# A fused attention and mixture-of-experts kernel: longer weight rows, early weights spread over the row tiles, and another order of expert loads

## The chip, the cores and the metric

The kernel runs on one core of a Trainium2 chip. The metric is device time in microseconds (us) of one execution; lower is better.

## The reference

Chunked attention feeds a mixture of experts with a capacity. The shapes are q, k, v: 8 x 8 x 576 x 64; x: 4608 x 512; w1: 8 x 512 x 1024; w2: 8 x 1024 x 512; capacity 80; all in float32.

```python
scores = scale * np.matmul(q_c, k_c.transpose(0, 1, 2, 4, 3))   # chunks of 64
attn = softmax(scores)
x = np.matmul(attn, v_c)                     # as 4608 rows of 512
logits = x @ w_gate
expert_idx = np.argmax(logits, axis=1)
gate_w = softmax(logits)[its own expert]
out = np.zeros((N, D))
for e in range(8):
    tok_idx = the 80 rows of expert e with the largest gate_w
    h = np.maximum(x[tok_idx] @ w1[e], 0.0)
    out[tok_idx] = gate_w[tok_idx, None] * (h @ w2[e])
```

So at most 640 of the 4608 rows of the output are not zero, but all 32 MB of expert weights (4 MB an expert) have to come in, and all of the output (9.4 MB) has to be written.

## The kernel before

**Attention.** The 4608 rows are 36 row tiles of 128. The loop at L1043 is software pipelined by hand: in turn i it does `scores(i)` (L387), `probs(i - 1)` (L420), `values(i - 2)` (L431), `finish(i - 2)` (L497) and `xtrans(i - 3)` (L520). Loads of q and k (`load_qk`, L376, 0.5 MB a tile, 7 buffers) and v (`load_v`, L369, 5 buffers) stand on SyncE's queue (SP), which issues in program order: what waits there holds up all that stands behind it. Every four tiles x is written to a scratch array `xs` in DRAM from GpSimd's queue (POOL).

**Lists.** For each expert the kernel finds a threshold, ranks the kept rows and makes a list of row numbers. For experts 0 and 1 a first list is made from tiles 0 to 23 alone (`first_list`, L792). Three one-hot tiles `ohS` (L843) on VectorE (DVE) are multiplied with `comp` in 24 small matmuls on TensorE (PE) into `liS` (`pe_list`, L852); `rows_` (L859) reads the row numbers from it and gathers 128 rows of `xs` by an indirect DMA (`gather`, L174). That is group 0. Its transposes (L928) and its first and second products with the weights of experts 0 and 1 (`first_group`, L922, tiles `h0` and `y0`) fill PE while the other lists are made after the loop. `first_q` and `pe1` are queues of small steps, of which the loop does one now and then (`burst`, L330; `step_one`, L318).

**Experts.** The other lists are five groups of 128 slots, each of four chunks of 32 slots, in `CHUNKS` (L46): group 1 holds experts 0 and 2, group 2 experts 1 and 3, group 3 experts 4 and 5, group 4 experts 5 and 6, group 5 experts 6 and 7. `place` (L148) makes the row numbers: `gi1` for group 1, then `gi2` for the other four. `experts` (L203) gathers the rows of each group, and for each does `xpose` (transposes), `layer1` in two halves (L222: 32 matmuls each, the instruction line is L185 in `product1`), `hpose` and `layer2` (64 matmuls, L193 in `product2`). Its order on PE from group 2 on is: first half of layer 1 of group r, `hpose` of r-1, `xpose` of r+1, second half of layer 1 of r, layer 2 of r-1. The result is scaled on DVE (L252) and scattered to the output by an indirect DMA (`store`, L198); the stores wait for each other and for all `clear`s (L287), nine DMAs of 1 MB that write zeros over the output.

**Weights.** `w1` of an expert is loaded as 128 partitions x 4 rows of 4 KB. `w2` is loaded as 128 partitions x 8 rows of 2 KB. The weights of experts 0 and 1 come in eight pieces of 1 MB (numbers 0 to 3: expert 0, first weights in two halves, then second weights; 4 to 7: expert 1), issued in the turns that the table `EARLY` (L42) gives (`early_weights`, L964). After the loop the DMA `hold` (L1094) waits for `tS`, which GpSimd makes behind the first gather's issue (L886), so that no later weights are issued before that gather. Then follow the loads of experts 2 to 7 and the clears (`part`, L1289; `ahead`, L1300; L1318 to L1323). `part(3, 1)` waits for a DVE copy into the buffer (L1295), which itself waits for `gi2` and stands on DVE behind the scaling of group 0.

**Buffers.** The pool `wp` has two buffers each for first and second weights (experts 0 and 1, then 5 and 6); `wp2` has six for either kind (experts 2, 3, 4, then 7). A load into a used buffer waits for the matmuls that read it last. `room` (L1282) chooses the pool:

```python
pool = wp if e in (5, 6) else wp2
for e, l in {0: ((3, 1), (4, 0), (4, 1)), 1: ((5, 0),),
             2: ((5, 1),), 3: ((6, 1), (7, 1))}.get(r, ()):
```

Here l = 0 is an expert's first weights and l = 1 its second. In turn 2 the last four clears, (6, 0) and (7, 0) follow.

Of the kernel before, what the change touches and what calls it, by code (L numbers as in the profile page):

```python
# [8 lines left out]
F32 = mybir.dt.float32  # L9
BF16 = mybir.dt.bfloat16  # L10
I32 = mybir.dt.int32
# [6 lines left out]
P = 128  # L18
# [5 lines left out]
NT = 9  # L24
# [14 lines left out]
LAG = 2  # L39
HOT = 8  # L40

EARLY = {6: [0], 14: [1], 28: [2, 3], 29: [4], 30: [5], 31: [6], 32: [7]}  # L42
VLOGITS = {28: (0,), 29: (1,), 33: (2, 3)}
FIRST = 24
FS = 64
# [22 lines left out]
def attention_moe(ctx: ExitStack, tc: tile.TileContext, qk, vv, v8, vt, wg, w1, w2, cap, cst, hst, out):  # L68
# [26 lines left out]
    slot_oob = cp.tile([P, NR], F32, name="slot_oob")  # L95
    flag_i = cp.tile([P, 1], I32, name="flag_i")

    def tiles_w(pool, e, tag=""):
        one = pool is not wp
        return (pool.tile([P, 4, FF], F32, name=f"w1_{tag}{e}", tag="w" if one else "w1"),  # L100
                pool.tile([P, 8, DM], F32, name=f"w2_{tag}{e}", tag="w" if one else "w2"))

    def load_w(pool, e, tag=""):
        a, b = tiles_w(pool, e, tag)
        nc.sync.dma_start(a, w1[e].rearrange("(c p) f -> p c f", p=P))
        nc.sync.dma_start(b, w2[e].rearrange("(c p) d -> p c d", p=P))
        return a, b

    mp = ctx.enter_context(tc.tile_pool(name="slots", bufs=1))
# [184 lines left out]
    with ExitStack() as actx:  # L294
# [35 lines left out]
        def burst(most=8):  # L330

            for _ in range(most):
                step_one(first_q)
# [458 lines left out]
        def first_list():  # L792
# [5 lines left out]
            c1S, pnS, thS, _ = const8("c1S"), const8("pnS"), const8("thS"), const8("rest", P)  # L798
            mS, iS, pS = (small(x, (2, FIRST), BF16) for x in ("mS", "iS", "pS"))
            tS = S['tS'] = small("tS", (2, FIRST))  # L800
            hot1 = []
            go = {}

            def emitted(nm, fn):
# [36 lines left out]
            def one_hot(j):  # L841
                oh = wk.tile([P, P, HOT], BF16, name=f"ohS{j}", tag="qk", bufs=NB)
                v.tensor_tensor(  # L843
                    oh.rearrange("p (e s) r -> p e s r", e=2),
                    S['io_s'].rearrange("p (e s) r -> p e s r", e=2),
                    pS[:, :, None, HOT * j:HOT * j + HOT].to_broadcast([P, 2, FS, HOT]),
                    op=ALU.is_equal)
                hot1.append(oh)
                if len(hot1) == FIRST // HOT:
                    emitted("list", pe_list)  # L850

            def pe_list():  # L852
                Z['liS'] = li = pa.tile([P, 6, 2], F32, name="liS", tag="acc")
                for rt in range(FIRST):
                    nc.tensor.matmul(li, lhsT=hot1[rt // HOT][:, :, rt % HOT],
                                     rhs=comp[:, rt, :, 0:2],
                                     start=rt == 0, stop=rt == FIRST - 1)

            def rows_():  # L859
# [104 lines left out]
        def early_weights(n):  # L964

            e, c = divmod(n, 4)
            if c == 0:
                weights[e] = tiles_w(wp, e)
            j = c % 2
            w, src, m = ((weights[e][0], w1, 2), (weights[e][1], w2, 4))[c // 2]  # L970
            nc.sync.dma_start(
                w[:, m * j:m * j + m],
                src[e].rearrange("(c p) f -> p c f", p=P)[:, m * j:m * j + m])

        with tc.manual_schedule():
            load_qk(0)
# [66 lines left out]
            for i in range(RT - 1):  # L1043
                if i == 6:
                    late_constants()
                S['i'] = i
                scores(i)
                j = i - 4
                due = j >= 0 and j % 4 == 3
                if due:  # L1050
                    gate_mm(j - 3, 4)
                    gate_copy(j - 3, 4)
                if i >= 1:
                    probs(i - 1)
                    if i == 1:
                        warm_up(8)
                if i >= 2:
                    values(i - 2)
                    burst()
                    finish(i - 2)  # L1060
                pe_slot()
                if i == 34:
                    step_one(pe1)
                if i >= 2:
                    for r in VLOGITS.get(i, ()):
                        value_logits(r)
                if due:
                    gate_sum(j - 3, 4)
                    gates.append((group_done, (j // 4,)))
                if i >= 3:  # L1070
                    xtrans(i - 3)
                pe_slot()
                if i < 33:
                    step_one(pe1)
                if i == 21:
                    nc.sync.dma_start(S['vT'], vt)
                if i == 25:
                    nc.sync.dma_start(vh, v8)
                if i == 30:
                    S['io_s'] = wk.tile([P, P, HOT], BF16, name="io_s", tag="qk", bufs=NB)  # L1080
                    nc.scalar.copy(S['io_s'].rearrange("p (e s) r -> p e s r", e=2),
                                   io_b[:, None, 0:FS, None].to_broadcast([P, 2, FS, HOT]))
                if i >= 2 and i - 2 + NB < RT:
                    load_qk(i - 2 + NB)
                if i >= 2 and i - 2 + NV < RT:
                    load_v(i - 2 + NV)
                for n in EARLY.get(i, ()):
                    early_weights(n)
# [3 lines left out]
            assert 'xg0' in S  # L1092
            hold = mp.tile([P, 2], F32, name="hold")
            nc.sync.dma_start(hold, S['tS'][:, 0, 0:2])  # L1094
            scores(35)
            gate_mm(28, 4)
            gate_copy(28, 4)
# [125 lines left out]
                select(e)  # L1223
            ahead_first(1)
            pl1, gi1 = place(mp, ps2, "g", sel_part, cb, "c", CHUNKS[:1])
            ahead_first(4)
            halves_ = slice(0, FS), slice(FS, P)
            nL = small("nL", (1,))
            for e, q in enumerate(halves_):
# [46 lines left out]
    with tc.manual_schedule():  # L1276
        with ExitStack() as ectx:
# [4 lines left out]
            def room(e, l):  # L1282

                w = weights.setdefault(e, [None, None])
                pool = wp if e in (5, 6) else wp2
                w[l] = pool.tile([P, *((4, FF), (8, DM))[l]], F32, name=f"w{l + 1}_{e}",
                                 tag=f"w{l + 1}" if pool is wp else "w")

            def part(e, l, after=None):  # L1289
# [3 lines left out]
                w = weights[e][l]  # L1293
                if after is not None:
                    nc.vector.tensor_copy(w[:, 0, 0:1], after)  # L1295
                nc.sync.dma_start(w, (w1, w2)[l][e].rearrange("(c p) f -> p c f", p=P))

            stored = []

            def ahead(r, xg, scale, ys):  # L1300

                if r == 0:
                    ahead_first(RT)
                    scale(0, S_y0)
                for e, l in {0: ((3, 1), (4, 0), (4, 1)), 1: ((5, 0),),
                             2: ((5, 1),), 3: ((6, 1), (7, 1))}.get(r, ()):
                    part(e, l, S_gi2[:, 0:1] if (e, l) == (3, 1) else None)
                if r == 2:
                    for n in range(5, NT):
                        clear(n)  # L1310
                    part(6, 0)
                    part(7, 0)
                if r >= 2:
                    for j in sorted(set(ys) - set(stored)):
                        store(ys[j], si[:, j:j + 1])
# [2 lines left out]
            room(2, 1)  # L1318
            part(2, 0)
            part(2, 1)  # L1320
            for n in range(5):
                clear(n)
            part(3, 0)  # L1323
            experts(ep, pp, lambda r: gi1[:, 0:1] if r == 1 else gi2[:, r - 2:r - 1], si, gate_t,
                    weights.get, "c", CHUNKS, ahead)
# [139 lines left out]
def _arrays(q, k, v, moe_w_gate, moe_w1, moe_w2, moe_capacity):  # L1465
# [12 lines left out]
        e[..., 0:64].transpose(1, 4, 0, 3, 2).reshape(P, 4, 8, 64))  # L1478
    r["wg"] = np.ascontiguousarray(moe_w_gate)
    r["w1"] = np.ascontiguousarray(moe_w1)  # L1480
    r["w2"] = np.ascontiguousarray(moe_w2)
    r["cap"] = np.asarray(moe_capacity, np.int64).reshape(1).view(np.int32).reshape(1, 2)
    r["cst"] = _constants()
    r["hst"] = _hist()
# [18 lines left out]
```

## Time and profile before

| | |
|---|---|
| time, median of 3 runs | 262.15 us (262.05 to 265.08) |
| profiled execution, its own time | 262.55 us |
| its span (first to last instruction) | 260.8 us |
| TensorE busy | 232.0 us, 89% of the span |
| TensorE weight load busy (beside it) | 131.8 us |
| VectorE, ScalarE, GpSimd busy | 135.1, 77.6, 49.3 us |
| mean granted TensorE clock | 0.953 of 2.4 GHz |
| DMA traffic | 86.17 MB, mean 330 GB/s |

The profile is one execution, with all times in us from its first instruction. PE is TensorE's matmul, PEld its weight load, DVE VectorE, ACT ScalarE, POOL GpSimd, SP SyncE; a q behind an engine's name means its instruction queue, which issues DMAs. "Idle <-X" is the time for which the engine stood still just before an instruction, and what released it. A clock of 1.00 is 2.4 GHz and 0.50 is 1.2 GHz. MB and GB here are powers of ten, KB are 1024 bytes: a weight load of 2048 KB is 2.10 MB.

### The profile page before, as it was taken

How to read it: one execution, taken by the hardware profiler on the slowest of the kernel's cores; microseconds unless marked ns; L12 is line 12 of the kernel's file. 1: busy time of each engine (PE TensorE's matmuls, PEld its weight loads, DVE VectorE, ACT ScalarE, POOL GpSimd, SP SyncE). 2: the span in 40 equal slices, each digit the busy share in tenths (PEclk: the TensorE clock that was granted, in tenths of full speed). 3: DMA queues.
4: the chain of work that ended last, by engine and by line, in shares of the span. 5: the costliest groups of instructions: out<-in, count | busy, mean ns of one | idle time of the engine just before them, and what ended most of it. 6: DMA issues, size and time to landing. Idle time of an engine off the chain costs nothing. (4 is left out here: it accounts for less than half of the span.)

```text
span 260.8 us, 8075 instructions
## 1 busy us (share of the span) xinstructions
PE 232.0 (89%) x3441; PEld 131.8 (51%) x3441; DVE 135.1 (52%) x429; ACT 77.6 (30%) x167; POOL 49.3 (19%) x127
## 2 busy tenths in 40 slices
PE   7699999999999999999988866999779949999970
PEld 5576767676767678778543522333114213333310
DVE  4688796969696997889486683112102101121210
ACT  2134445455554357533453401111002002010000
POOL 4003130303030483014351016000000011110110
PEclk9999999999999999997799995899979979999996
DMA  7899999999999999999999999799899999910011
GB/s 243 275 385 316 371 410 412 357 393 409 406 355 374 405 371 362 330 415 398 399 374 402 407 412 410 240 403 392 329 322 406 412 418 396 381 52 0 3 38 36
DMA packets 32665, 86.17 MB, mean 330 GB/s; under 512 B 3375, under 2 KB 3631, under 8 KB 32368
## 3 DMA queue, kind: packets, MB, share of 16 engines
q1 hardware_dynamic: 28912, 72.69, 74.9%
q0 software_dynamic: 3424, 12.32, 11.8%
q10 hardware_dynamic: 288, 0.59, 0.8%
q8 instruction: 29, 0.48, 0.7%
q14 instruction: 12, 0.10, 0.1%
HBM read 65.40 MB, written 20.45 MB: 329 GB/s over the span
## 5 line engine op out<-in xcount | busy, mean ns | idle before, releaser
L185 PE MATMUL hc<-w,xtc 128*32 128x512 f32 x320 | 42.0, 645 | 6.7 <-DMA w<-in_w 6.7
L454 PE MATMUL o<-vb,pT 128*64 128x130 f32 x512 | 35.4, 279 | 0.1
L193 PE MATMUL yc<-w,htc 128*32 128x512 f32 x320 | 35.3, 592 | 0.0
L401 DVE TENSOR_REDUCE mx<-s 128x8 f32<-128x512 f32 x36 | 24.7, 687 | 12.8 <-PE s L395 12.7
L454 PEld LDWEIGHTS o<-vb,pT 128*64 128x64 f32 x512 | 27.6, 135 | 5.5 <-issue 4.2
L427 ACT ACTIVATE pT<-pt 128x512 f32<-128x512 f32 x36 | 21.5, 598 | 25.3 <-PE pt L425 25.0
L395 PE MATMUL s<-qk 64*64 64x64 f32 x1152 | 25.9, 227 | 3.2 <-issue 1.6
L185 PEld LDWEIGHTS hc<-w,xtc 128*32 128x32 f32 x320 | 10.8, 117 | 34.2 <-issue 25.6
L524 ACT COPY xT<-px 128x512 f32<-128x512 f32 x32 | 18.8, 586 | 26.5 <-PE px L416 26.3
L404 DVE TENSOR_TENSOR sm<-s,mx 128x512 f32<-128x512 f32 x36 | 24.8, 690 | 0.7
L482 DVE TENSOR_TENSOR x<-o,rc 128x512 f32<-128x512 f32 x36 | 24.8, 688 | 0.6
L425 PE MATMUL pt<-ct,sm 128*128 128x128 f32 x144 | 23.7, 287 | 1.1
L395 PEld LDWEIGHTS s<-qk 64*64 64x64 f32 x1152 | 20.9, 136 | 6.8 <-issue 2.6
L229 ACT ACTIVATE hsc<-hc 128x512 f32<-128x512 f32 x5 | 3.0, 598 | 65.7 <-PE hc L185 65.7
L199 POOL DMA_INDIRECT out<-ysc,si x6 | 5.9, 988 | 87.3 <-issue 46.9
L193 PEld LDWEIGHTS yc<-w,htc 128*32 128x32 f32 x320 | 10.3, 110 | 23.5 <-issue 23.5
L425 PEld LDWEIGHTS pt<-ct,sm 128*128 128x128 f32 x144 | 15.1, 140 | 11.8 <-issue 5.8
L494 POOL DMA_DIRECT2D xs<-x x8 | 6.7, 832 | 72.4 <-DVE keys L590 50.0
L246 DVE COPY htc<-hpc 128x512 f32<-128x512 f32 x5 | 3.5, 692 | 30.4 <-PE hpc L242 30.4
L252 DVE TENSOR_SCALAR ysc<-yc,gate 128x512 f32<-128x512 f32 x5 | 3.8, 751 | 27.4 <-PE yc L193 27.4
L416 PE MATMUL px<-ct,x 64*128 64x64 f32 x256 | 15.3, 238 | 0.1
L231 DVE TENSOR_SCALAR hsc<-hc 128x512 f32<-128x512 f32 x5 | 3.5, 691 | 20.5 <-PE hc L185 20.5
(218 smaller groups left out, 259.8 us busy)
## 6 DMA issues: line engine op xcount, KB each, us to landing
w<-in_w SPq DMA_DIRECT2D x12, 2048.0 KB, 16.1
qk<-in_qk SPq DMA_DIRECT2D x35, 512.0 KB, 7.7
out<-zero SPq DMA_DIRECT2D x9, 1024.0 KB, 14.8
vb<-in_vv SPq DMA_DIRECT2D x64, 130.0 KB, 6.8
xs<-x POOLq DMA_DIRECT2D x8, 1024.0 KB, 10.5
w<-in_w SPq DMA_DIRECT2D x8, 1024.0 KB, 13.4
vh<-in_v SPq DMA_DIRECT2D x1, 1168.0 KB, 7.8
vT<-in_vt SPq DMA_DIRECT2D x1, 1024.0 KB, 6.9
```

What stands on the lines that cost most here:

```text
L185: nc.tensor.matmul(h[o:o + 32, :], lhsT=xT[:, b, o:o + 32], rhs=getw(e)[0][:, b, 512 * f:512 * f + 512], start=(b == 0), stop=(b == 3), ti ...
L193: nc.tensor.matmul(y[o:o + 32, :], lhsT=hT[c // 4][:, c % 4, o:o + 32], rhs=getw(e)[1][:, c, :], start=(c == 0), stop=(c == 7), tile_posit ...
L395: nc.tensor.matmul(ps[64 * u:64 * u + 64, h, 64 * pr:64 * pr + 64], lhsT=t['q'][64 * h:64 * h + 64, pr, u, :], rhs=t['k'][64 * h:64 * h + ...
L401: nc.vector.tensor_reduce(mx, s8, axis=AX.X, op=ALU.max)
L404: nc.vector.tensor_tensor(sm.rearrange("p c h k -> p h c k" if T == 8 else "p c k h -> p h c k"), s8, mx[:, :, :, None].to_broadcast([P, 2 ...
L416: nc.tensor.transpose(pm[:, u, 64 * pr:64 * pr + 64], src(pr)[rows], ident[rows, rows])
L425: nc.tensor.transpose(pt[:, pr, :], sv[:, pr, :], ident)
L427: nc.scalar.activation(pT, pt, AF.Exp, scale=0.125)
L454: nc.tensor.matmul(po[64 * u:64 * u + 64, pr // 2, o:o + 130].rearrange("p (h x) -> p h x", h=2), lhsT=d['pT'][:, pr, 64 * u:64 * u + 64], ...
L482: nc.vector.tensor_tensor(t['x'][:, r, :].rearrange("p (m j e) -> p j m e" if T == 8 else "p (j m e) -> p j m e", j=2, m=4), U[i]['pov'][. ...
L494: nc.gpsimd.dma_start(xs[T * 512:T * 512 + 512].rearrange("(c p) d -> p c d", p=P), t['x'])
L524: nc.scalar.copy(t['xT'][:, :, P * r:P * r + P].rearrange("p a (u j) -> p a u j", u=2), pm)
```

## The change

1. The array `w2` is laid out in DRAM so that each partition's rows j and j+1 lie side by side: the same tile is loaded as 4 rows of 4 KB instead of 8 of 2 KB.
2. The table `EARLY` spreads the eight early pieces: expert 1's first weights (4 and 5) go to turns 18 and 24, its second weights (6 and 7) behind `hold`.
3. The 24 list products are issued in three parts of eight, each when its one-hot tile is made, ahead of `probs(33)`, `values(32)` and behind them.
4. A new DMA `held` on SP waits for `mark`, a copy of `gi1` on ACT; expert 3's first weights stand behind it. The wait of (3, 1) for `gi2` is gone, and one clear of the first five goes to the last.
5. The second weights of expert 5 go to a buffer of `wp2`, and the order of the last loads and clears is another.

```diff
-EARLY = {6: [0], 14: [1], 28: [2, 3], 29: [4], 30: [5], 31: [6], 32: [7]}
+EARLY = {6: [0], 12: [1], 18: [4], 24: [5], 28: [2], 30: [3], 35: [6, 7]}
...
+    def source(l, e):
+        return (w1[e].rearrange("(c p) f -> p c f", p=P) if l == 0 else
+                w2[e].rearrange("c p j d -> p c (j d)"))
+    def wide(l, t):
+        return t.rearrange("p (c j) d -> p c (j d)", j=2) if l else t
...
-                hot1.append(oh)
-                if len(hot1) == FIRST // HOT:
-                    emitted("list", pe_list)
+                if j == 0:
+                    Z['liS'] = pa.tile([P, 6, 2], F32, name="liS", tag="acc")
+                emitted("list", lambda: pe_list(j, oh))
...
                 scores(i)
+                if i == 34:
+                    step_one(pe1)
...
                 if i >= 2:
+                    if i == 34:
+                        step_one(pe1)
                     values(i - 2)
+                    if i == 34:
+                        step_one(pe1)
                     burst()
                     finish(i - 2)
                 pe_slot()
-                if i == 34:
-                    step_one(pe1)
...
             nc.sync.dma_start(hold, S['tS'][:, 0, 0:2])
+            for n in EARLY[35]:
+                early_weights(n)
...
             pl1, gi1 = place(mp, ps2, "g", sel_part, cb, "c", CHUNKS[:1])
-            ahead_first(4)
+            ahead_first(2)
+            mark = mp.tile([P, 1], I32, name="mark")
+            nc.scalar.copy(mark, gi1)
+            ahead_first(2)
...
-                pool = wp if e in (5, 6) else wp2
+                pool = wp2 if e not in (5, 6) or (e, l) == (5, 1) else wp
...
-                for e, l in {0: ((3, 1), (4, 0), (4, 1)), 1: ((5, 0),),
-                             2: ((5, 1),), 3: ((6, 1), (7, 1))}.get(r, ()):
-                    part(e, l, S_gi2[:, 0:1] if (e, l) == (3, 1) else None)
+                for e, l in {0: ((3, 1), (4, 0), (4, 1)), 1: ((5, 0), (5, 1)),
+                             2: ((6, 0), (6, 1), (7, 0))}.get(r, ()):
+                    part(e, l)
                 if r == 2:
-                    for n in range(5, NT):
+                    for n in range(4, NT):
                         clear(n)
-                    part(6, 0)
-                    part(7, 0)
+                    part(7, 1)
...
-            for n in range(5):
+            for n in range(4):
                 clear(n)
+            held = mp.tile([P, 1], I32, name="held")
+            nc.sync.dma_start(held, mark)
             part(3, 0)
...
-    r["w2"] = np.ascontiguousarray(moe_w2)
+    r["w2"] = np.ascontiguousarray(np.asarray(moe_w2).reshape(NE, 4, 2, P, DM).swapaxes(2, 3))
```

The order of SP's queue around `hold`, before (w1_1 is an array of first weights, here expert 1's; w2 second weights; qk the loads of q and k; out<-zero the clears):

```order
L971 DMA w2_0_542<-in_w2 128x4x512 x2
L385 DMA qk34_2251<-in_qk 128x1024
L971 DMA w1_1_2253<-in_w1 128x2x1024
L385 DMA qk35_2320<-in_qk 128x1024
L971 DMA w1_1_2253<-in_w1 128x2x1024
L971 DMA w2_1_2254<-in_w2 128x4x512 x2
L1094 DMA hold_2685<-tS_2165 128x2
```

and now:

```order
L977 DMA w2_0_542<-in_w2 128x2x1024
L394 DMA qk34_2254<-in_qk 128x1024
L394 DMA qk35_2320<-in_qk 128x1024
L977 DMA w2_0_542<-in_w2 128x2x1024
L1103 DMA hold_2683<-tS_2168 128x2
L977 DMA w2_1_1363<-in_w2 128x2x1024 x2
```

Six early pieces stood between tile 33's loads and `hold`; now two do, and two follow `hold`. The other two (w1_1) stand some ten tiles earlier.

SP's queue from expert 3's first weights to its end, before:

```order
L1296 DMA w1_3_3208<-in_w1 128x4x1024
L1296 DMA w2_3_3249<-in_w2 128x8x512
L1296 DMA w1_4_3252<-in_w1 128x4x1024
L1296 DMA w2_4_3254<-in_w2 128x8x512
L1296 DMA w1_5_3300<-in_w1 128x4x1024
L1296 DMA w2_5_3395<-in_w2 128x8x512
L290 DMA out_0<-zero_75 512x1x512 x4
L1296 DMA w1_6_3401<-in_w1 128x4x1024
L1296 DMA w1_7_3403<-in_w1 128x4x1024
L1296 DMA w2_6_3504<-in_w2 128x8x512
L1296 DMA w2_7_3506<-in_w2 128x8x512
```

and now:

```order
L1337 DMA held_3209<-mark_3092 128x1
L1310 DMA w1_3_3211<-in_w1 128x4x1024
L1310 DMA w2_3_3252<-in_w2 128x4x1024
L1310 DMA w1_4_3254<-in_w1 128x4x1024
L1310 DMA w2_4_3256<-in_w2 128x4x1024
L1310 DMA w1_5_3302<-in_w1 128x4x1024
L1310 DMA w2_5_3304<-in_w2 128x4x1024
L1310 DMA w1_6_3399<-in_w1 128x4x1024
L1310 DMA w2_6_3401<-in_w2 128x4x1024
L1310 DMA w1_7_3403<-in_w1 128x4x1024
L299 DMA out_0<-zero_75 512x1x512 x5
L1310 DMA w2_7_3410<-in_w2 128x4x1024
```

Expert 6's first weights stood behind four clears and now stand ahead of all that are left; the last clears move behind three more loads, and one clear more is among them.

PE's queue around the list products in turn 34, before (s34, pt33 and o32 are the scores, transposes and values of tiles 34, 33 and 32):

```order
L395 MATMUL s34_2576<-qk34_2251 64x64 x16
L425 MATMUL pt33_2597<-ct_64,sm33_2489 128x128 x4
L444 MATMUL o32_2611<-vh_118,pT32_2506 64x73 x16
L855 LDWEIGHTS ohS0_2517
L855 MATMUL liS_2636<-comp_77,ohS0_2517 128x12
```

and now:

```order
L404 MATMUL s34_2575<-qk34_2254 64x64 x16
L862 LDWEIGHTS ohS0_2515
L862 MATMUL liS_2517<-comp_77,ohS0_2515 128x12
...
L434 MATMUL pt33_2604<-ct_64,sm33_2487 128x128 x4
L862 LDWEIGHTS ohS1_2518
L862 MATMUL liS_2517<-comp_77,ohS1_2518 128x12
...
L453 MATMUL o32_2626<-vh_118,pT32_2504 64x73 x16
```

Sixteen of the 24 products move ahead of o32, and the last eight stay behind it.

## Rows read from the trace of the kernel before

**Rows 1.** The page: the span, and the costliest group of instructions
```profile
span 260.8 us, 8075 instructions
...
L185 PE MATMUL hc<-w,xtc 128*32 128x512 f32 x320 | 42.0, 645 | 6.7 <-DMA w<-in_w 6.7
```

**Rows 2.** Timeline, PE, expert stage: start, us taken, line, names, shape, count [idle <-releaser]
```profile
186.71 1.03 PE L185 MATMUL hc<-w,xtc 128*32 128x512 f32 x6
190.64 5.32 PE L185 MATMUL hc<-w,xtc 128*32 128x512 f32 x26 [2.90 <-DMA w<-in_w]
...
212.51 5.15 PE L185 MATMUL hc<-w,xtc 128*32 128x512 f32 x28 [3.81 <-DMA w<-in_w]
...
219.05 3.64 PE L185 MATMUL hc<-w,xtc 128*32 128x512 f32 x32
...
241.97 10.51 PE L193 MATMUL yc<-w,htc 128*32 128x512 f32 x96
```

**Rows 3.** Busy us (xcount) of PE, PEld, DVE, ACT, POOL; PE clock, DMA share, GB/s
```profile
60.00:101.00 41.00, 40.28 (x814) 29.90 (x810) 34.51 (x123) 21.57 (x49) 14.99 (x43) 1.00 1.02 388
...
164.00:168.00 4.00, 4.00 (x40) 1.30 (x36) 0.27 (x2) 0.46 (x1) 0.00 (x0) 0.95 0.66 177
187.00:190.00 3.00, 0.74 (x6) 0.00 (x0) 0.74 (x1) 0.00 (x0) 0.00 (x0) 1.00 0.73 193
...
195.20:207.00 11.80, 11.80 (x106) 4.31 (x108) 1.39 (x2) 1.77 (x3) 0.00 (x0) 1.00 1.05 409
208.00:212.00 4.00, 0.70 (x4) 0.00 (x0) 0.70 (x1) 0.00 (x0) 1.03 (x1) 1.00 1.02 414
212.20:215.60 3.40, 3.09 (x16) 0.79 (x20) 0.00 (x0) 0.00 (x0) 0.24 (x1) 0.50 1.03 421
224.00:227.00 3.00, 3.00 (x32) 0.91 (x28) 0.00 (x0) 0.00 (x0) 0.00 (x0) 1.00 1.05 388
```

**Rows 4.** Waits of SP's queue: who <- whom: us in total, times, longest
```profile
SPq L1296 <- PE yc L193: 17.6, 2, 11.1
...
SPq L1296 <- DVE w L1295: 13.1, 1, 13.1
```

**Rows 5.** Timeline, SP: `hold`, then (5, 0) and (5, 1)
```profile
125.82 0.51 SPq L1094 DMA_DIRECT2D hold<-tS  x1
...
171.57 4.21 SPq L1296 DMA_DIRECT2D w<-in_w  x1
...
186.90 0.37 SPq L1296 DMA_DIRECT2D w<-in_w  x1
```

**Rows 6.** DMA issues at 171.6 and at 186.9: count, size, us from issue to landing
```profile
w<-in_w SPq DMA_DIRECT2D x1, 2048.0 KB, 19.0
...
w<-in_w SPq DMA_DIRECT2D x1, 2048.0 KB, 9.9
```

**Rows 7.** Timeline, PE: the list products, and the first gather's transposes
```profile
121.65 1.65 PE L855 MATMUL liS<-comp,ohS 128*128 128x12 bf16 x24
...
131.62 0.63 PE L928 MATMUL xp<-ct,xg 128*128 128x128 f32 x4 [1.47 <-DMA xg<-xs,gi]
```

**Rows 8.** Waits of PE's attention loop for q and k, whole run
```profile
PE s L395 <- DMA qk<-in_qk: 1.4, 3, 0.6
```

**Rows 9.** Timeline, POOL: group 1's gather; the first, second and last store
```profile
152.08 1.10 POOL L176 DMA_INDIRECT xgc<-xs,gic  x1 [8.00 <-DVE some L1240]
...
208.29 1.03 POOL L199 DMA_INDIRECT out<-ysc,si  x1 [46.93 <-issue]
215.36 1.00 POOL L199 DMA_INDIRECT out<-ysc,si  x1 [6.05 <-DMA out<-ysc,si]
...
253.58 0.97 POOL L199 DMA_INDIRECT out<-ysc,si  x1 [5.89 <-DVE ysc L252]
```

**Rows 10.** DMA issues at 208.3 and at 230.7: stores, us from issue to landing
```profile
out<-ysc,si POOLq DMA_INDIRECT x1, 6.3
...
out<-ysc,si POOLq DMA_INDIRECT x1, 2.7
```

More of the change, by code (lines that the diff above doesn't have):

```diff
@@ L105, in load_w @@
         nc.sync.dma_start(a, w1[e].rearrange("(c p) f -> p c f", p=P))
-        nc.sync.dma_start(b, w2[e].rearrange("(c p) d -> p c d", p=P))
+        nc.sync.dma_start(wide(1, b), source(1, e))
         return a, b
@@ L800, in first_list @@
             tS = S['tS'] = small("tS", (2, FIRST))
-            hot1 = []
             go = {}
@@ L847, in one_hot, with pe_list @@
                     op=ALU.is_equal)
-                hot1.append(oh)
-                if len(hot1) == FIRST // HOT:
-                    emitted("list", pe_list)
[L852 to L856, printed above, removed]
+                if j == 0:
+                    Z['liS'] = pa.tile([P, 6, 2], F32, name="liS", tag="acc")
+                emitted("list", lambda: pe_list(j, oh))
+            def pe_list(j, oh):
+                for rt in range(HOT * j, HOT * j + HOT):
+                    nc.tensor.matmul(Z['liS'], lhsT=oh[:, :, rt % HOT], rhs=comp[:, rt, :, 0:2],
                                      start=rt == 0, stop=rt == FIRST - 1)
@@ L969, in early_weights @@
             j = c % 2
[L970 to L973, printed above, removed]
+            l = c // 2
+            nc.sync.dma_start(wide(l, weights[e][l])[:, 2 * j:2 * j + 2],
+                              source(l, e)[:, 2 * j:2 * j + 2])
         with tc.manual_schedule():
@@ L1295, in part @@
                     nc.vector.tensor_copy(w[:, 0, 0:1], after)
-                nc.sync.dma_start(w, (w1, w2)[l][e].rearrange("(c p) f -> p c f", p=P))
+                nc.sync.dma_start(wide(l, w), source(l, e))
             stored = []
```

## The prediction

> **What bounds the kernel now.** I read the page first: its costliest group is the first product, with 6.7 us of idle time in front of it, all on weight loads [rows 1]. PE is busy 89% of the span, so the next view is PE's timeline in the expert stage: where are those 6.7 us? In two places [rows 2]. The first half of layer 1 of group 3 stops after 6 of its 32 matmuls and waits 2.90 us for (5, 0). The first half for group 4 stops after 4 and waits 3.81 us for (6, 0). Each wait costs more than itself. An undisturbed half takes 3.64 us for 32 matmuls, so 26 would take 2.96; after the first wait they took 5.32, which is 2.36 more. The 28 after the second should take 3.19 and took 5.15, 1.96 more. The windows say why: from 212.2 to 215.6 the granted clock was 0.50, the 1.2 GHz level, after PE had stood still [rows 3]. The two stops therefore cost 5.26 and 5.77 us. From the second one PE runs on to 252.48 (241.97 + 10.51); then comes the last scaling and store at 253.58 [rows 9], and the span ends at 260.8.
>
> Why are the loads late? The windows show two holes in the stream of transfers: 177 GB/s at 164 to 168 and 193 at 187 to 190, beside 409 to 421 in full stretches [rows 3]. SP's waits name them: 13.1 us on the DVE copy in front of (3, 1), and 11.1 us (the longer of two) on layer 2 of group 1, whose buffer (5, 1) needs [rows 4]. (5, 0) was issued at 171.57 and landed 19.0 us later, at 190.6 [rows 5, 6]: it stood behind other transfers, so it is the stream that was late, not its issue. (6, 0) stood behind four clears.
>
> **The change part by part.** Sums are against the profiled execution (262.55 us, of which the span is 260.8). It lies 0.4 above the median of 262.15, so I take 0.4 off at the end.
>
> *Rows of 4 KB.* Loads of 4 KB rows moved at 414 GB/s, loads of 2 KB rows at 388 [rows 3]. A load of 2.10 MB then takes 5.07 us rather than 5.41. Four such loads (expert 1's to 4's) stand ahead of (5, 0): 1.3 us. The bounds are 0 and 1.4.
> The Trainium skill ("DMA: Bandwidth & Descriptors", Specifications) gives 512 B as the transfer from which a DMA reaches line rate. By that rule both forms would be equal and this term 0; the two windows differ by 26 GB/s, which speaks against it, though other transfers lay in them too. It is rival B.
>
> *Early weights.* Pieces 4 and 5, 2.1 MB, move into turns 18 and 24. PE is busy 40.28 of 41 us from 60 to 101, and the engines move 388 GB/s there [rows 3]. At 414 they could move 1.07 MB more; the other 1.03 MB, 2.5 us, must come out of what is loaded ahead, and seven buffers of 0.5 MB hold 3.5 MB. PE waited for q or k only 1.4 us in the whole loop [rows 8], so I cost it at nothing; what it costs without that cover is rival C.
> Only two pieces then stand between turn 28 and `hold`, so the queue runs empty before the first gather. Its 1.47 us wait on PE [rows 7] should mostly go: I take 1.2, between 0.3 (only the smaller part) and 1.47. The values of the last tile stand behind that gather's transposes on PE, so the final lists, group 1's gather (152.08, [rows 9]) and all of the expert stage move with it.
>
> *List products in three parts.* 16 of the 24 move ahead of o32. The 24 take 1.65 us [rows 7], so o32 and DVE's work behind it come up to 1.1 us later, and with them perhaps the list, the gather's issue and `hold`. The bounds are 0 (the products no longer wait for the third one-hot tile) and 1.1. I take 1.1: `hold` at 126.9 instead of 125.82 [rows 5], the first load behind it at 127.5.
>
> *The restart.* Behind `hold` an empty queue has to get going. No row shows this. Nearest from above: (5, 1), issued into the hole at 187, took 9.9 us [rows 6], which is 4.5 beyond 5.4 of moving. From below: a store of 0.26 MB on idle engines took 2.7 [rows 10], 2.1 beyond its 0.6. I take the middle, 3.3. Pieces 6 and 7 (2.10 MB, 5.1 us) then have landed at 127.5 + 3.3 + 5.1 = 135.9.
>
> *`held`, and (3, 1) without its cast.* `mark` is a copy of one column on ACT, which I cost at nothing: ACT is busy 77.6 of 260.8 us. `held` waits for it near 152, just before the gather's issue [rows 9], while two loads and four clears behind piece 7, 8.4 MB, keep the queue busy until 135.9 + 20.5 = 156.4; so I cost it at nothing too, and if the clears ran out earlier, each us of gap makes the later loads 1 us later. Queued behind it on SP are expert 3's loads and all later ones. The 13.1 us wait of (3, 1) goes, and the hole at 164 with it. The one clear that moves from the first five to the end is worth 2.6 us of stream ahead of (5, 0).
>
> *Buffers and order.* (5, 1) now needs the buffer of expert 2's first weights, which is free after layer 1 of group 1 rather than layer 2: the hole at 187 goes. (6, 0) comes second behind (5, 0), without clears between.
>
> *Sum.* From 135.9 to the landing of (5, 0) the engines move seven loads (14.68 MB), four clears (4.19), the last x rows (1.05) and five gathers (1.31): 21.2 MB. At 410 GB/s, as from 195.2 to 207 [rows 3], that is 51.8 us: (5, 0) lands at 187.7 instead of 190.6. PE comes to it at 187.74 − 1.2 = 186.5 and waits 1.2 instead of 2.90. It goes on 2.9 us earlier, and of the slow matmuls' 2.36 I take half back, 1.2 (bounds 0 and 2.36). The second stop goes altogether: (6, 0) lands two loads later, 187.7 + 10.2 = 197.9. PE needed it at 208.7 (212.51 − 3.81) before, some 204.6 now, so there are 6.7 us to spare. Sum: −2.9 − 1.2 − 5.8 = −9.9, that is 252.65 for a profiled execution, **252.3 us** against the median.
>
> What is late next? The stores, which wait for all clears. Behind (5, 0) come four loads and five clears, 13.63 MB: the last clear lands at 187.7 + 33.2 = 220.9. The first store, 1.0 us behind it, takes 6.3 beside the last load [rows 10] and 0.8 until the next is issued (215.36 − 208.29 − 6.3, [rows 9]); four more at 2.7 + 0.8. The sixth can go 22.1 us after the last clear, at 243.0. PE has its result ready at 253.58 − 9.9 = 243.7. That is a margin of 0.7 us only, and each us by which clears come later costs one.
>
> Own range: with the restart at 2.1, 414 GB/s and no list delay, (5, 0) lands at 126.4 + 2.1 + 5.1 + 51.2 = 184.8, before PE comes, and both stops go: −1.2 − 2.9 − 2.36 − 5.77 = −12.2, about 250; with PE's start moved by 1.47 and a little of group 1's gather too, 249. With 4.5 and 400 GB/s it lands at 190.1: −0.5 − 5.8, about 255.9.
>
> **The rivals.**
> *A: the stream is no faster.* 388 GB/s throughout, as in both windows with mixed transfers [rows 3], and a restart of 4.5: pieces 6 and 7 land at 137.4, (5, 0) at 137.4 + 54.7 = 192.1. The first stop then ends 1.5 later, only the second goes: +1.5 − 5.8, or **257.9**. For it: the average over the span is 330 GB/s. Against: 409 to 421 where nothing waits.
> *B: 4 KB rows give nothing.* Without the 1.3 us (5, 0) lands at 189.0: −1.6 − 0.6 − 5.8 = −8.0, or **254.2**.
> *C: the loop pays for pieces 4 and 5.* If what was loaded ahead doesn't cover them, PE waits 2.6 us (1.05 MB at 400 GB/s) for one or both, and all behind moves: 252.3 + 2.6 or + 5.2, **254.9 to 257.5**. For it: 388 GB/s is near the top already. Against: the 1.4 us of [rows 8].
> *D, slower: the clears hold up the stores.* From 130.8 to the last clear 36.9 MB have to move (2.10 + 21.2 + 13.63). The sixth store was issued at 253.58; it would be later than that if the last clear landed after 253.58 − 22.1 = 231.5, which takes a mean rate below 36.9 / 100.7 = 367 GB/s. From that point each us counts. At 360 GB/s the last clear is at 233.3 and the time **264.0**. For it: clears go last, and holes of 177 and 193 GB/s exist. Against: both holes have a named cause that is removed.
> The Trainium skill ("DMA: Bandwidth & Descriptors", Specifications) puts the HBM limit of a core at about 358 GB/s, which speaks for D; this trace moves 388 to 421 in every full stretch of [rows 3], so I keep D's chance small.
>
> **How the numbers follow.** The forecast has 0.62, and a still better case near 249 has 0.02. A has 0.12, B 0.10, C 0.10, D 0.04. About 2% can be told from no change, so faster means below 256.9. The forecast's cases (0.62 + 0.02), B and half of C lie there: 0.79. A, the other half of C and a part of D are within 2%: 0.19. Above 267.4 only a bad D is left: 0.02. The range is 249 to 258.5: the forecast's own range is 249 to 255.9, and A and C lie up to 258; D is left out.
>
> **What would show it.** Right: no wait on a weight load in front of the first half for group 4, and one near 1 us for group 3; no row of SP for a DVE copy, and the one for layer 2 shorter; no window below 350 GB/s from 140 to 225; second weights moving near 410; less than 0.5 us ahead of xp. Wrong: a wait for q or k above 3 us (C); the last store waiting for the store before it instead of for DVE (D); (5, 0) landing after 190 (A); PE at 0.50 behind a stop that I have as gone.

## The result and the profile after

| | before | after |
|---|---|---|
| time, median of 4 runs | 262.42 us (262.05 to 265.08) | 253.84 us (252.79 to 254.55) |
| ratio, 95% interval | | 0.965 (0.958 to 0.972) |
| profiled execution, its span | 262.55, 260.8 us | 252.79, 251.0 us |

The prediction was 252.3 us (249 to 258.5); the measured median lies 1.5 us above it and inside the range. The kernel before, run again beside the experiments, took between 257.6 and 265.2 us, and for five of the runs below no interval could be worked out; they are given with their spread alone. The profiled execution is the fastest of the four; against the one of before it gained 9.8 us. PE reached the first half of group 3 4.2 us earlier (186.71 to 182.48), lost 0.8 more in that half, and was 6.4 us faster in the first half of group 4. The page of the changed kernel has the same group at its head as [rows 1], now with one stop instead of two:

```profile
span 251.0 us, 8078 instructions
...
L194 PE MATMUL hc<-w,xtc 128*32 128x512 f32 x320 | 38.5, 613 | 4.0 <-DMA w<-in_w 4.0
```

PE's timeline of the changed kernel answers to [rows 2, 7] (start, us taken, line, names, shape, count, idle time and its releaser):

```profile
127.54 0.63 PE L934 MATMUL xp<-ct,xg 128*128 128x128 f32 x4 [0.52 <-DVE sh L576]
...
155.07 1.11 PE L226 MATMUL xpc<-ct,xgc 128*128 128x128 f32 x4 [3.14 <-DMA xgc<-xs,gic]
...
182.48 1.03 PE L194 MATMUL hc<-w,xtc 128*32 128x512 f32 x6
187.54 4.99 PE L194 MATMUL hc<-w,xtc 128*32 128x512 f32 x26 [4.02 <-DMA w<-in_w]
...
204.24 3.62 PE L194 MATMUL hc<-w,xtc 128*32 128x512 f32 x32
...
232.16 10.51 PE L202 MATMUL yc<-w,htc 128*32 128x512 f32 x96
```

Three things are to be seen. The half at 204.24 (layer 1 of group 4) runs its 32 matmuls in 3.62 us without a wait: the second stop is gone. (5, 0) landed at 187.5, as forecast (187.7). But PE came to it at 183.5, 3 us earlier than forecast, and so stood still for 4.02 us, longer than before. PE ends at 232.16 + 10.51 = 242.67, against 252.48.

The windows of the changed kernel (us; busy us and count of PE, PEld, DVE, ACT, POOL; granted clock, DMA share, GB/s) answer to [rows 3]:

```profile
117.00:120.00 3.00, 3.00 (x88) 2.85 (x87) 2.97 (x10) 0.86 (x2) 1.80 (x4) 1.00 0.04 10
124.00:127.00 3.00, 3.00 (x77) 2.44 (x77) 2.10 (x7) 2.01 (x4) 1.39 (x4) 1.00 0.49 131
164.00:168.00 4.00, 4.00 (x40) 1.24 (x36) 0.50 (x1) 0.44 (x1) 0.00 (x0) 1.00 1.03 412
170.00:180.00 10.00, 10.00 (x96) 3.75 (x92) 1.38 (x2) 1.73 (x3) 0.00 (x0) 1.00 1.03 408
187.50:190.90 3.40, 3.36 (x20) 0.91 (x24) 0.00 (x0) 0.00 (x0) 0.00 (x0) 0.59 1.03 412
```

The holes at 164 and at 187 are closed (412 GB/s, where [rows 3] have 177 and 193). A new one is open ahead of the first gather: 10 GB/s at 117 to 120, 131 at 124 to 127. And the stop at 183.5 is followed by a mean clock of 0.59, most of that stretch at the 1.2 GHz level, as [rows 3] show it behind a stop of before.

Between 140 and 220 no window of 10 us moves less than 404 GB/s, and no wait of SP for a DVE copy is left; its wait for layer 2 has shrunk from 11.1 to 4.3 us.

GpSimd's timeline shows the stores, first, second, fifth and sixth, beside [rows 9]:

```profile
221.55 1.03 POOL L208 DMA_INDIRECT out<-ysc,si  x1 [64.26 <-SPq L1345]
227.09 1.00 POOL L208 DMA_INDIRECT out<-ysc,si  x1 [4.51 <-DMA out<-ysc,si]
...
237.41 0.98 POOL L208 DMA_INDIRECT out<-ysc,si  x1 [2.46 <-DVE ysc L261]
243.77 0.97 POOL L208 DMA_INDIRECT out<-ysc,si  x1 [5.38 <-DVE ysc L261]
```

The first went 0.9 behind the last clear (220.6; the forecast was 220.9). The sixth still waited for DVE, so for PE's result, and not for the store before it.

### The profile page after: what moved, and what is told of

The parts are those of the page before. It is cut to its first block, busy times and chain, and to the rows that moved or that the text cites. A ratio compares the mean times of both kernels' runs of the same rounds, so it can differ in the third digit from the quotient of the medians.

```text
span 251.0 us, 8078 instructions
## 1 busy us (share of the span) xinstructions
PE 226.6 (90%) x3441; PEld 130.6 (52%) x3441; DVE 134.6 (54%) x428; ACT 77.7 (31%) x168; POOL 49.2 (20%) x127
## 5 line engine op out<-in xcount | busy, mean ns | idle before, releaser
L194 PE MATMUL hc<-w,xtc 128*32 128x512 f32 x320 | 38.5, 613 | 4.0 <-DMA w<-in_w 4.0
L404 PE MATMUL s<-qk 64*64 64x64 f32 x1152 | 25.0, 224 | 1.8 <-issue 1.6
L404 PEld LDWEIGHTS s<-qk 64*64 64x64 f32 x1152 | 20.1, 134 | 5.1 <-issue 2.8
```

The costliest lines, as they stand in the source:

```text
L194: nc.tensor.matmul(h[o:o + 32, :], lhsT=xT[:, b, o:o + 32], rhs=getw(e)[0][:, b, 512 * f:512 * f + 512], start=(b == 0), stop=(b == 3), ti ...
L404: nc.tensor.matmul(ps[64 * u:64 * u + 64, h, 64 * pr:64 * pr + 64], lhsT=t['q'][64 * h:64 * h + 64, pr, u, :], rhs=t['k'][64 * h:64 * h + ...
```

## The experiments

Two theories stood behind the choice of runs. **S**: the stream of transfers sets the end, by the landing of (5, 0) and (6, 0) and by the last clear; PE's own earlier work is worth nothing while it stands in front of (5, 0). **P**: PE's own path sets it; the 4.1 us by which the first gather's transposes start earlier (127.54 against 131.62) are what was gained. Each experiment undoes one part in the changed kernel, or does one part alone in the kernel before.

### The order of the last loads and the buffers, alone and undone

```diff
# b_order: in the kernel before
-                pool = wp if e in (5, 6) else wp2
+                pool = wp2 if e not in (5, 6) or (e, l) == (5, 1) else wp
...
-                for e, l in {0: ((3, 1), (4, 0), (4, 1)), 1: ((5, 0),),
-                             2: ((5, 1),), 3: ((6, 1), (7, 1))}.get(r, ()):
+                for e, l in {0: ((3, 1), (4, 0), (4, 1)), 1: ((5, 0), (5, 1)),
+                             2: ((6, 0), (6, 1), (7, 0))}.get(r, ()):
...
-                    part(6, 0)
-                    part(7, 0)
+                    part(7, 1)
# a_order_old: the same lines the other way, in the changed kernel
```

Expected, alone: 

> The kernel before with the new buffers and the new order of the last loads alone. S: (5, 0) stays at 190.6 with its stop of 2.9 us, the second stop goes with its slow stretch: 5.8 us less, 256 to 258 us. Rival (the second stop was paid by the stream as a whole, and needs the earlier parts of the change as well): 260 to 262.5 us.

Expected, undone: 

> The changed kernel with the old buffers and the old order of the last loads: (5, 1) waits for layer 2 of group 1, five clears stand ahead of (6, 0). S: (5, 0) stays at 187.5, (6, 0) lands some 24 us behind it at 211 to 212, PE stops 7 to 8 us in front of group 4's first half and loses 2 more at half clock: 262 to 264 us, all of the gain. Rival: only the old second stop comes back (3.8 + 2.0): 259 to 260 us.

Measured: alone 255.0 us (253.6 to 255.8), undone 262.67 us (261.4 to 265.0). PE's timeline of the first, at the first halves of groups 3 and 4:

```profile
190.01 5.32 PE L185 MATMUL hc<-w,xtc 128*32 128x512 f32 x26 [3.03 <-DMA w<-in_w]
...
207.04 3.62 PE L185 MATMUL hc<-w,xtc 128*32 128x512 f32 x32
```

and of the second:

```profile
206.56 1.03 PE L194 MATMUL hc<-w,xtc 128*32 128x512 f32 x4
211.16 5.32 PE L194 MATMUL hc<-w,xtc 128*32 128x512 f32 x28 [3.57 <-DMA w<-in_w]
```

In the first, the stop for (5, 0) stays just as it was (3.03 us, 5.32 for the 26) and the one for group 4 is gone, which is what S says; the time is 1 us below its range. In the second, group 4's stop is back. The time is that of S, but the stop is 3.57 and not 7 to 8 us: (6, 0) landed at 211.1 as expected, only PE came to it later than I had worked out (at 207.6), because it had left the first stop later and slower (26 matmuls in 6.58 us from 188.27). So this one part carries nearly all: 7.4 us below the median of before when done alone, 8.8 us lost when undone. What the other four parts add together cannot be told from no change: 255.0 (253.6 to 255.8) without them, 253.84 (252.8 to 254.6) with them. The two halves of this part, the buffer of (5, 1) and the order of the loads, were not run apart, so which of them carries the gain is not shown.

### The early weights

```diff
# a_early_old: in the changed kernel
-EARLY = {6: [0], 12: [1], 18: [4], 24: [5], 28: [2], 30: [3], 35: [6, 7]}
+EARLY = {6: [0], 14: [1], 28: [2, 3], 29: [4], 30: [5], 31: [6], 32: [7], 35: []}
# b_early: the new table, and its two pieces behind hold, in the kernel before
```

Expected, old table in the changed kernel: 

> The changed kernel with the old table of early weights (all eight pieces ahead of `hold`). Theory S (the stream of transfers sets the end: PE waits 4.02 us for (5, 0), which lands at 187.5, so what ends earlier on PE ahead of that is worth nothing): the queue no longer runs empty from 115 to 127, 2.1 MB less stand behind `hold`, (5, 0) lands 4 to 5 us earlier (182.5 to 183.5) and the stop shrinks below 2 us even if the loop ends later: 248 to 251 us. Theory P (the change gained by ending the loop 4.1 us earlier on PE, which the spread table brought): the loop ends 1 to 4 us later again and the time is 254 to 258 us.

Expected, new table in the kernel before: 

> The kernel before with the new table of early weights alone. S: two pieces of 1 MB behind `hold` put (5, 0) some 5 us later, to 194 to 196, and the time 3 to 5 us above before: 265 to 268 us; the loop ends earlier, to no avail. P: the loop's end 1 to 4 us earlier is kept to the end: 258 to 261 us.

Measured: the old table makes the changed kernel **faster**, 250.26 us (248.9 to 251.5), ratio 0.950 (0.944 to 0.956) against before, an interval below that of the changed kernel. The new table alone leaves the kernel before where it was: 263.7 us (260.6 to 267.3), ratio 0.999 (0.995 to 1.004). The window ahead of the first gather, with the old table in the changed kernel:

```profile
117.00:120.00 3.00, 3.00 (x98) 2.74 (x96) 2.95 (x9) 0.54 (x3) 1.81 (x3) 1.00 1.03 416
```

PE's stop for (5, 0) in the same run:

```profile
185.88 3.62 PE L194 MATMUL hc<-w,xtc 128*32 128x512 f32 x26 [2.81 <-DMA w<-in_w]
```

and GpSimd's last two stores in it:

```profile
237.34 0.98 POOL L208 DMA_INDIRECT out<-ysc,si  x1 [2.46 <-issue]
242.30 0.98 POOL L208 DMA_INDIRECT out<-ysc,si  x1 [3.98 <-issue]
```

With six pieces ahead of `hold` the engines are full at 117 to 120 (416 GB/s beside 10), and nothing of expert 1's is left behind it. The first gather landed at 130.0 instead of 127.4, and PE came to (5, 0) at 183.1, no later than in the changed kernel. Part of that delay went into a shorter wait for group 1's gather (1.46 instead of 3.14), and behind the shorter wait the clock stayed at 1.00, where the changed kernel had 0.50 from 155 to 159. The same 16 matmuls just behind that gather's transposes, first in the changed kernel and then with the old table, show it:

```profile
156.12 3.63 PE L202 MATMUL y<-w,hT 128*32 128x512 f32 x16
```

```profile
156.57 1.92 PE L202 MATMUL y<-w,hT 128*32 128x512 f32 x16
```

The sixth store now waits for the fifth (landed at 241.5), no longer for PE. (5, 0) landed at 185.8, 1.7 earlier. S had 4 to 5, but the queue lost part of that again: `hold` was issued at 126.65 instead of 125.22, and the first load behind it took 10.7 us to land. S's time (248 to 251) came out and P's 254 to 258 is out. But of the 3.0 us by which PE ends earlier in the profiled execution (239.65 instead of 242.67), only 1.7 are the landing; the other 1.4 are the 26 matmuls at full clock (3.62 instead of 4.99), which S did not foresee.

For b_early both theories missed: the time neither rose by 3 to 5 us nor fell. Its trace is of the slowest of its ten executions (267.33 us) and cannot explain the median. It has (5, 0) at 192.9, ahead of S's 194 to 196, no hole at 164 to 168 (424 GB/s), and a new stop of 3.62 us for (3, 0), which landed at 171.9.

### The list products

```diff
# a_list_one: the changed kernel with the 24 products in one part, behind o32
# b_list: the kernel before with the three parts of eight
+                if j == 0:
+                    Z['liS'] = pa.tile([P, 6, 2], F32, name="liS", tag="acc")
+                emitted("list", lambda: pe_list(j, oh))
```

Expected: 

> The changed kernel with the 24 list products in one part, behind o32. S: the first gather's transposes may start up to 4 us later (the granted clock at 120 to 127 shows whether the split had anything to do with that stretch), but (5, 0) still lands within 1 us of 187.5 and the time is within 1 us of the changed kernel's median of 253.8. P: as much later as the loop ends, 1 to 4 us: 254.8 to 257.8 us.

and 

> The kernel before with the list products in three parts alone. S: within 1 us of before, 261.4 to 263.4, whatever the loop's end does: PE comes earlier to the same wait for (5, 0). P: 1 to 4 us less, 258.4 to 261.4. If the split is what took the stretch of half clock at 120 to 127 away, it is at 1.00 here; if the emptier queue did, it is at 0.5 here and at 1.00 with the new table alone.

Measured: 254.27 us (ratio to before 0.970, 0.963 to 0.977) and 263.7 us (1.003, 0.998 to 1.009). Neither is told from its base, 253.84 us for the first and a ratio of 1 for the second: the split is worth nothing that a run can show, as S says, although 263.7 lies 0.3 above the range given for it. Nor did `hold` move by the 1.1 us that I had charged: without the split it was issued at 125.4 in the changed kernel, with it at 125.2. The granted clock at 120 to 127 is 1.00 in both. PE's wait for the first gather in b_list is longer than the 1.47 us of [rows 7]:

```profile
131.04 0.63 PE L925 MATMUL xp<-ct,xg 128*128 128x128 f32 x4 [2.44 <-DMA xg<-xs,gi]
```

### The copy that (3, 1) waited for

```diff
# a_cast, in the changed kernel
-            mark = mp.tile([P, 1], I32, name="mark")
-            nc.scalar.copy(mark, gi1)
...
-                    part(e, l)
+                    part(e, l, S_gi2[:, 0:1] if (e, l) == (3, 1) else None)
...
-            held = mp.tile([P, 1], I32, name="held")
-            nc.sync.dma_start(held, mark)
```

Expected: 

> The changed kernel without `held` and `mark`, with (3, 1) waiting for the DVE copy behind gi2 again; four clears stay first. S: the hole at 164 to 168 comes back (4 us at 177 instead of 410 GB/s, 2.3 us), (5, 0) lands at 189.5 to 190.5 and the time goes up by 2 to 3 us; group 1's gather comes in behind (3, 0) and 3 to 5 us later, which PE's stop covers. P: that gather alone decides and the time goes up by 3 to 5 us with (5, 0) no later than 188.

Measured: 254.04 us (252.7 to 257.1), not told from the changed kernel; (5, 0) landed at 187.8, and group 1's gather at 155.3 instead of 155.0. A row of SP's waits in that run (us in total, times, longest) shows that the wait itself is back:

```profile
SPq L1308 <- DVE w L1307: 12.0, 1, 12.0
```

together with its window where the hole was:

```profile
164.00:168.00 4.00, 4.00 (x40) 1.48 (x40) 0.00 (x0) 1.07 (x2) 0.00 (x0) 1.00 1.03 411
```

The wait is back at 12.0 us, close to the 13.1 of [rows 4], and yet there is no hole: (3, 1) was issued at 161.0, while (3, 0) and the gathers were still coming in until 167.4. Both theories missed this. What closed the hole at 164 is not `held`: with two early pieces behind `hold`, the stream itself runs later, and the same wait ends before the queue is empty. In b_order, without these pieces, the hole is there (238 GB/s in the same window). The time from the landing of (3, 0) to that of the load behind it says the same of all kernels with this wait: 9.0 us in the kernel before (5.9 when it was run again), 7.8 in b_order and 11.4 in b_list, but 5.4 in b_early, which has the new table alone, and 5.1 in a_cast.

### Rows of 2 KB

```diff
# a_rows2k, in the changed kernel
-                w2[e].rearrange("c p j d -> p c (j d)"))
+                w2[e].rearrange("(c p) d -> p c d", p=P))
...
-    r["w2"] = np.ascontiguousarray(np.asarray(moe_w2).reshape(NE, 4, 2, P, DM).swapaxes(2, 3))
+    r["w2"] = np.ascontiguousarray(moe_w2)
```

Expected: 

> The changed kernel with second weights in rows of 2 KB again. If the longer rows are worth 0.34 us a load (388 against 414 GB/s), the four such loads ahead of (5, 0) put its landing from 187.5 to 188.8, the stop from 4.0 to 5.3 and the time up by 1.3 us. If both forms move alike (rival B), all three stay within 0.4 us.

Measured: 256.56 us (256.2 to 257.8), 2.7 above the changed kernel (252.8 to 254.6), without an interval. A load of second weights landed 5.4 us behind the one ahead of it, in the changed kernel 5.1, as the forecast had it (5.41 and 5.07); loads of first weights, in rows of 4 KB in both kernels, took 5.1 in this run too. From the last early piece to (5, 0) took 51.55 us instead of 50.61: 0.9 us for three such loads. The window at 170 to 180 has 398 GB/s where the changed kernel has 408:

```profile
170.00:180.00 10.00, 10.00 (x96) 3.96 (x92) 2.08 (x3) 1.74 (x3) 0.00 (x0) 1.00 1.04 398
```

Rival B is out. The rest of the 2.7 us is not settled. In the profiled execution, the slowest of the four, `hold` came 1.6 us later, behind a stretch of half clock that v_fill2 has too, with rows of 4 KB (see the end), and the 26 matmuls behind the stop took 6.57 us instead of 4.99.

### Clears moved: is the stream the bound, and are the stores next?

```diff
# v_later2, in the changed kernel
-                    for n in range(4, NT):
+                    for n in range(2, NT):
...
-            for n in range(4):
+            for n in range(2):
# v_mix, in v_later2: (7, 0) and the clears ahead of (6, 1) and (7, 1)
-                             2: ((6, 0), (6, 1), (7, 0))}.get(r, ()):
+                             2: ((6, 0), (7, 0))}.get(r, ()):
...
+                    part(6, 1)
                     part(7, 1)
# v_fill2, in the changed kernel: two of the first four clears in turn 34
+                if i == 34:
+                    clear(0)
+                    clear(1)
...
-            for n in range(4):
+            for n in range(2, 4):
```

Expected of v_later2: 

> The changed kernel with two of the first four clears moved to the last (seven last). S: (5, 0) lands two clears earlier, at 182.3, before PE comes at 183.5: the stop of 4.0 and the 2.0 of slow matmuls go. But the last clear still lands at 220.6, so the sixth store cannot go before 240.9, while PE's result is ready at 237.7 (mechanism of rival D): 2.9 us less, 250 to 251.5 us, and the last store waits for the store before it. If the stores are no limit: 6 us less, 247 to 248.5 us.

Expected of v_mix: 

> The kernel of v_later2 with (7, 0) and all seven clears ahead of (6, 1) and (7, 1). If the stores behind the last clear are what limits v_later2 (its sixth store went at 243.3, 0.8 behind the landing of the fifth, while PE's result was ready at 238.7), the last clear lands one load earlier, at 216.8, and the sixth store can go 2.5 to 4.6 us earlier: 247 to 249.2 us. (6, 1) lands at 221.9, 0.6 before PE needs it at 222.5. If the stores are no limit, or two loads behind the clears slow the first stores by as much, it stays at 251 to 252 us.

Expected of v_fill2: 

> The changed kernel with two of the first four clears issued in turn 34, into the empty queue ahead of the first gather (rows of after: 10 GB/s at 117 to 120). S: they land by 123, when that gather is issued; all that follows lands 5 us earlier, (5, 0) at 182.3 and the last clear at 215.4; no stop, stores no limit: 6 us less, 247 to 248.5 us. Rival (whatever stands ahead of the first gather holds up lists and PE): the gather lands 4 to 5 us later, PE with it, and the time stays at 252 to 255 us.

Measured: 251.56 us (251.2 to 253.5; ratio 0.964, 0.956 to 0.973), 251.11 us (249.6 to 252.0; ratio 0.972, 0.965 to 0.980, against executions of the kernel before of 257.6 to 261.3 us, so a gain of 2% is not clear in this one) and 250.66 us (249.9 to 251.9; 0.959, 0.951 to 0.967). PE's timeline of v_later2 at group 3's first half:

```profile
183.82 3.62 PE L194 MATMUL hc<-w,xtc 128*32 128x512 f32 x32
```

and its last two stores:

```profile
239.64 0.98 POOL L208 DMA_INDIRECT out<-ysc,si  x1 [3.46 <-DVEq L1345]
243.34 0.97 POOL L208 DMA_INDIRECT out<-ysc,si  x1 [2.72 <-issue]
```

(5, 0) landed at 183.0, the stop is gone, PE runs 32 matmuls in 3.62 us and is done at 237.6, 5.1 us earlier. But the sixth store still went at 243.34, 0.4 earlier than in the changed kernel: it waited for the fifth, which landed at 242.6. That is the mechanism of rival D, shown as a bound, if not as a loss against before. In v_mix the last clear lands at 217.0 instead of 221.8 and the sixth store goes at 240.97; its profiled execution takes 249.55 us, but its median is within 0.5 of v_later2's, and so the 247 to 249.2 us forecast for it was missed. In v_fill2 the two clears fill the empty queue, but the first gather is issued 2.2 us later (125.36), in an execution with PE at 0.50 from 122 to 128, (5, 0) comes at 186.0 and the sixth store waits for the fifth too. Its 250.66 us lies between the two forecasts, 2 us above the one and 1 us below the other.

The two ways of easing the stream are not worth the same. Two clears (2.1 MB, 5.1 us at 410 GB/s) moved behind (5, 0) brought it 4.5 us earlier. The same 2.1 MB moved into the empty queue ahead of the gather brought 1.5 us (v_fill2) and 1.7 (a_early_old): `hold` then came 2.2 and 1.4 us later. Nor does the chain of stores keep its pace: the fifth store took 2.7 us to land in the changed kernel and 4.1 to 4.5 in a_early_old, v_mix and v_fill2. Why is open.

### The kernel before, once more

Expected: 

> The kernel before once more, for its granted clock at 120 to 127. If the stretch at 0.5 belongs to that program (its list products in one part or its full queue), it is there again; if it comes and goes between executions, it may be missing, and the first gather's transposes then still start near 131, because the gather lands behind the early weights.

Measured: 262.14 us. The granted clock is 1.00 from 116 to 130, the first gather landed at 129.2, and its transposes started at 130.4 without waiting for it. So the stretch at 0.50 comes and goes. The gather was not late behind the early weights as expected: the last of these had landed at 124.4, and PE itself came late (the product `poS` of the first list stands at 115.4, in the execution of [rows 7] at 113.9). The stops of 3.3 and 3.7 us are there.

The best median of all is that of a_early_old, the changed kernel with the old table of early weights; those of v_fill2, v_mix and v_later2 lie within 1.3 us of it, and their spreads overlap with its own.

## Why the prediction came out right, step by step

- **The second stop.** "The second stop goes altogether": right in cause, which b_order shows alone, and 0.6 too small in size. The half for group 4 took 9.99 us before (207.67 to 217.66) and takes 3.62 now: −6.4, not −5.8. The forecast had counted the wait and the 28 matmuls behind it, and not the four ahead of it, whose 1.03 us are 0.6 more than four matmuls need in an undisturbed half.
- **(5, 0) at 187.7.** It landed at 187.5, but in part by luck, for three errors cancel. `hold` came 0.6 earlier than before instead of 1.1 later, 1.7 off. From there to the last early piece it took 11.7 us instead of 9.0, so this piece landed 1.0 later than forecast (136.9 instead of 135.9). The stream behind it took 50.6 instead of 51.8 us. The first half of the last x rows (0.5 MB), which the forecast counted behind the last early piece, landed beside it at 137.5; at 410 GB/s that is 1.3 us, the whole of the last error and half of the one before. The rate itself, 410 GB/s, was right.
- **PE's way to it: the step that failed.** I took 1.2 us for the first gather's wait. The transposes started 4.1 us earlier (131.62 to 127.54), as the gather landed at 127.4 instead of 131.5. The 1.47 us of [rows 7] were only what was left of that wait: PE itself was late in that execution, because it ran at half clock from 120 on. In b_list, where it did not, PE waited 2.44 us for the same gather, which landed at 130.9; at 113.8 PE was level in the two (`poS`). A wait shows how much later the releaser is than the engine, not how late it is. The 4.1 us are a difference of two executions, though: against the kernel before run again (130.38, no wait) it is 2.8.
- **Why it did no harm.** PE's 3 us went into the stop, which grew from 2.90 to 4.02 instead of shrinking to 1.2. The restart depends on the landing alone, and that was right. The half clock behind it took 2.0 us (4.99 for 26 matmuls that should take 2.96), not the 1.2 that I had left, so 0.3 instead of 1.2 came back. The sum is −3.1 for the restart, −0.3 for the slow matmuls and −6.4 for the second stop: −9.8, forecast −9.9. That it comes so close is luck too: 0.9 too much for the slow matmuls stands against 0.2 and 0.6 too little for the other two.
- **The shares.** The sum was right, its reasons were not all. `held` and the copy: nothing that a run shows (a_cast). The early pieces "at nothing": undoing them gains 3.6 us by the medians in the changed kernel and 1.8 in the profiled executions, though alone they changed nothing in the kernel before; the queue that they leave empty is the new hole at 117. The list products: nothing, neither way. The rows of 4 KB: near the 0.34 us a load that I had taken.
- **The rivals.** A and B are out by the windows (408 to 412 GB/s, and 398 with short rows). C did not happen: no wait for q or k is among PE's larger ones, although two pieces more came in by 101 (405 GB/s from 60 to 101, where [rows 3] have 388). D's bound is real and 2.9 us away in the changed kernel (the fifth store landed at 240.1, the next could have gone at 240.9, and went at 243.77); it takes over as soon as PE's stop is removed or shortened.

## What to carry to other kernels

Where an engine stands in front of a late transfer, what the engine does earlier is worth nothing: follow the queue back from the transfer and count the bytes ahead of it, and undo each part of a change by itself before it is kept, since here one part of five carried the gain and undoing another made the kernel 3.6 us faster still. A queue left empty to let one small transfer pass is paid for at the next late load; look for the window with few GB/s, but do not expect all of it back: bytes taken out of the stream ahead of the load brought 4.5 of 5.1 us, the same bytes put into the empty window 1.5 to 1.7. When a stop is removed or shortened, work out the next chain in the same way: here the stores behind the last clear were 2.9 us away, and four versions ended on them.

## What was not expected of the hardware

The stretch of half clock near 120 to 129 comes and goes between executions and is not a matter of the kernel's list products or of its queue alone: it is in 3 of the 14 profiled executions, those of the kernel before (list products in one part, full queue), of a_rows2k (three parts, empty queue) and of v_fill2 (three parts, full queue), and not in the kernel before run again, nor in the changed one. In the profiled execution of a_rows2k the clock fell although PE had been busy for all of the 4 us before it and went on being busy (us, PE's busy us and count, clock, DMA share, GB/s):

```profile
118.00:120.00 2.00, 2.00 (x78) 1.00 0.06 18
120.00:122.00 2.00, 2.00 (x44) 0.91 0.00 0
122.00:124.00 2.00, 2.00 (x48) 0.50 0.70 268
```

Nor is each stop followed by it: behind 2.90 us in the kernel before, 26 matmuls took 5.32 us; behind 2.81 in a_early_old they took 3.62, at a clock of 1.00. The same goes for the wait for group 1's gather, 3.14 us with half clock behind it in the changed kernel and 1.46 without in a_early_old. What decides it stays open; no run here was made for it.
